# A fused attention, mixture and convolution kernel on one core: taps of the convolution by DMA, half banks for the first scores, no unread products, other numbers in the planner

## The chip, the cores and the metric

The kernel runs on one core of one Trainium2 chip. The metric is the device time of one execution in microseconds (us), lower is better. Three executions of the kernel before took 445.81, 446.19 and 446.75 us (median 446.19). The execution that the profiler recorded took 444.8 us, of which its trace spans 443.0 us.

A core has a matrix engine (PE; its weight loads are listed as PEld), a vector engine (DVE), a scalar engine (ACT), a general engine (POOL) and a queue engine (SP) that issues most DMAs. Each engine runs its own instructions in order and waits on semaphores for the others. PE's results land in PSUM, a memory of 8 banks; everything else lies in SBUF.

## The reference

Everything is float32: batch B = 4, H = 8 heads of 64, S = 576 tokens, 512 channels.

```python
def reference(**kw):
    x = attention(q, k, v)          # (4, 8, 576, 64), window of 64 keys
    x = x.transpose(0, 2, 1, 3).reshape(4, 576, 512)
    x = channel_mix(x); return gated_conv(x)

def attention(q, k, v):
    s = (q @ k.T) / 8               # masked: 0 <= query - key < 64, else -1e9
    s = s - s.max(-1); e = exp(s)
    return (e / (e.sum(-1) + 1e-9)) @ v

def channel_mix(x):
    xp = x shifted by one token (zero at the start of each batch)
    xk = mu_k * x + (1 - mu_k) * xp
    xr = mu_r * x + (1 - mu_r) * xp
    h = relu(xk @ w_k)              # 512 -> 1024
    return sigmoid(xr @ w_r) * ((h * h) @ w_v)

def gated_conv(x):
    gate = sigmoid(sum over k = 0..4 of conv_w[k] * x shifted by 4 - k tokens)
    return (gate * (x @ w_val)) @ w_out
```

## The kernel before, in words

**First stage.** The 2304 tokens are cut into five blocks t = 0..4 of 256, 512, 512, 512 and 512 tokens, and each block into four pairs of heads: 20 units, numbered u = 4t + pair. A unit goes through these steps: scores on PE (`qk`, L289), scaling and window mask on DVE (`mask`, L301), a fix for batch starts on POOL (L311), the row maximum on DVE (`top`, L319), the exponentials with their sums on ACT (`exp`, L325), reciprocal and scaling on DVE (L332, L334), transposes on PE (`tp`, L342), their copies to SBUF on ACT or DVE (`pt`, L348 and L349), the product with v on PE (`pv`, L355), and a copy of its result to the block's transposed x (L361, L362).

From x a block mixes four operands: for each half g of the channels and each of r and k, x is scaled (L393 on ACT, L398 on DVE), the shifted x is added (`xm`, L409 on DVE), and for the blocks after the first the sum is split into a rounded high part (L423 on ACT, L424 on DVE) and the rest as low part (L426 on DVE). Then come the products r (4 tiles), h (8 tiles) and v (4 tiles). In block 0 they are plain float32 products with 256 columns (L457); in blocks 1 to 4 each is three passes (high by high, high by low, low by high) of 512 columns (L439). The split operands of block 1 lie where block 0's weights lay (`wide_x`), so they can be written only when block 0's products are done. In block 0 the weights themselves are made ready on ACT and DVE (`words`, `weight`: L210 to L239).

**Second stage.** Batch by batch (b = 0..3): x is read back (`load`, L569), split into the operands of a seven-product scheme (`prep`, L594 to L604), multiplied by w_val (L672), the products are combined and multiplied by the gate (L684 to L718), the result is split into high and low parts (g0h, g0l, g1h, g1l: L423, L424, L426) and multiplied by w_out (L439, names `out`), and stored (L746, L747). The gate of a batch has for each half p of the channels: tap 0 on ACT (L624), the other taps on DVE (L626), and the sigmoid on ACT (L653). For the taps in `BY_DMA`, in batches 1 to 3, ACT scales the shifted x into a buffer `tt` instead (L632; two such buffers exist), and POOL issues a DMA that adds the buffer to the gate (L643); the taps on DVE come behind that addition.

**What sets the order.** All operations are registered with the class `Plan`, each with an engine (or a choice of two), an assumed duration, a rank and its dependencies. `run` simulates the engines with these durations and emits the operation that can start first, among near ties the one of lowest rank. The tables `RANK` and `ADJ` give the ranks. The engines then run their instructions in the emitted order. PSUM rings limit what may be in flight: one buffer of two banks for scores (`pq`), two banks for transposes and `pv` (`pa`), four for r, h and v (`pg`). Where the simulation finds PE without work for over 700 ns before the first r product, `fill` (L882 to L888) emits products of the identity with itself whose result nothing reads.

## Time and profile before

| what | value |
|---|---|
| three executions | 445.81, 446.19, 446.75 us |
| profiled execution | 444.8 us, span 443.0 us |
| PE | 424.6 us busy (96%), 3172 records |
| DVE | 326.6 us busy (74%), 474 records |
| ACT | 266.2 us busy (60%), 584 records |
| POOL | 22.4 us busy (5%) |
| chain that ended last | PE 71%, DVE 20%, issue 3%, DMA 3%, ACT 2% |
| granted TensorE clock | mean 1.0 of full speed |

The busy time of an engine is the union of its records. The chain is followed back from the last instruction, at each step to what released it. Records of one engine overlap a little, so that the distance from one start to the next is a few hundredths of a microsecond less than a duration.

### The profile page before, as it was taken

To read this page: it belongs to the slowest core of one execution; us is meant where nothing else is said; L and a number is where in the kernel's file an instruction comes from. 1 tells how busy PE (TensorE), PEld (TensorE's weight loads), DVE (VectorE), ACT (ScalarE), POOL (GpSimd) and SP (SyncE) were. 2 spreads that over 40 slices of the span, in tenths; PEclk is the share of its full clock that TensorE was granted. 3 is DMA by queue.
4 is the path that set the end of the run, shared out by engine and by line. 5 is a ranking of instruction groups with operands and counts; after the bars stand their busy time and mean duration, and the time that the engine had idled before them with its cause. 6 is when DMAs were issued, how large, how long until landed. Compare 5 with 4: busy or idle time off the path is not lost.

```text
span 443.0 us, 7915 instructions
## 1 busy us (share of the span) xinstructions
PE 424.6 (96%) x3172; PEld 362.1 (82%) x3172; DVE 326.6 (74%) x474; ACT 266.2 (60%) x584; POOL 22.4 (5%) x69
## 2 busy tenths in 40 slices
PE   6879999899999999999999999999999799999996
PEld 4668788778878888888888878888889799899996
DVE  3999999998496149588147277765992899999950
ACT  4799987777546257896138553366430877685321
POOL 2001010011010001000000000000000001010000
PEclk9999999999999999999999999999999999999999
DMA  8998551602230143210121007300426426552022
GB/s 302 415 371 300 211 176 58 209 8 65 70 106 24 55 167 106 83 57 25 48 73 48 0 1 255 124 14 0 139 99 208 108 56 134 187 120 95 28 108 80
DMA packets 16692, 52.44 MB, mean 118 GB/s; under 512 B 1936, under 2 KB 2704, under 8 KB 15120
## 3 DMA queue, kind: packets, MB, share of 16 engines
q1 hardware_dynamic: 14928, 42.10, 27.5%
q0 software_dynamic: 864, 3.54, 4.0%
q10 hardware_dynamic: 864, 6.29, 3.8%
q8 instruction: 25, 0.41, 0.4%
q14 instruction: 11, 0.09, 0.1%
HBM read 38.95 MB, written 9.44 MB: 109 GB/s over the span
## 4 chain that ended last, share of the span: by engine, by line
PE 71%; DVE 20%; issue 3%; DMA 3%; ACT 2%; POOL 1%; ACTq 0%; POOLq 0%
PE h L439 20%; PE v L439 20%; PE r L439 9%; PE out L439 8%; PE qk L289 3%; PE at L355 3%; DMA xb<-x2d 3%; PE at L342 3%; PE val3m L672 3%; DVE x L604 2%; DVE m L319 2%; DVE words L215 2%; DVE s L301 2%; DVE s L334 1%; DVE xt L594 1%
## 5 line engine op out<-in xcount | busy, mean ns | idle before, releaser
L439 PE MATMUL h<-x,wk 128*128 128x512 f32 x384 | 91.3, 393 | 0.0
L439 PEld LDWEIGHTS h<-x,wk 128*128 128x128 f32 x384 | 71.0, 188 | 14.6
L439 PE MATMUL v<-sh,wv 128*128 128x512 f32 x256 | 80.5, 391 | 0.0
L325 ACT ACTIVATE s<-s,m 128x128 f32<-128x128 f32 x144 | 55.8, 388 | 12.4 <-DVE m L319 12.2
L439 PEld LDWEIGHTS v<-sh,wv 128*128 128x128 f32 x256 | 48.1, 188 | 10.3 <-issue 0.3
L439 PE MATMUL v<-sl,wv 128*128 128x512 f32 x128 | 49.9, 390 | 0.0
L439 PE MATMUL r<-x,wr 128*128 128x512 f32 x192 | 47.2, 397 | 0.7 <-DVE x L426 0.7
L439 PEld LDWEIGHTS r<-x,wr 128*128 128x128 f32 x192 | 35.1, 188 | 8.8 <-DVE x L426 1.1
L626 DVE SCALAR_TENSOR_TENSOR gate<-xb,wc,gate 128x576 f32<-128x576 f32 x52 | 39.5, 810 | 0.0
L516 DVE TENSOR_TENSOR sl<-rk,sh 128x1024 fp32r<-128x1024 f32 x16 | 19.5, 1222 | 21.7 <-ACT rk L514 21.7
L485 ACT ACTIVATE rk<-h 128x512 f32<-128x512 f32 (+1 forms) x35 | 19.3, 560 | 26.4 <-PE h L439 25.7
L301 DVE SCALAR_TENSOR_TENSOR s<-qk,cap 128x1024 f32<-128x1024 f32 (+1 forms) x24 | 22.5, 953 | 14.9 <-PE qk L289 8.7
L539 DVE TENSOR_TENSOR sgs<-v,sgs 128x512 f32<-128x512 f32 (+1 forms) x20 | 12.7, 635 | 25.7 <-PE v L439 25.7
L439 PEld LDWEIGHTS v<-sl,wv 128*128 128x128 f32 x128 | 24.0, 188 | 4.8
L439 PE MATMUL out<-g0h,wr 128*128 128x288 f32 x128 | 27.4, 295 | 0.0
L439 PE MATMUL out<-g1h,wr 128*128 128x288 f32 x128 | 27.2, 295 | 0.0
L355 PEld LDWEIGHTS at<-pt,vt 128*64 128x64 f32 x576 | 19.9, 137 | 8.6 <-issue 3.8
L325 ACT ACTIVATION_READ_ACCUMULATOR s<-s,m 128x1 f32 x144 | 26.9, 187 | 0.0
L355 PE MATMUL at<-pt,vt 128*64 128x64 f32 x576 | 23.6, 226 | 2.3 <-ACT pt L348 1.9
L409 DVE SCALAR_TENSOR_TENSOR xm<-xT,omu,xm 128x320 f32<-128x320 f32 (+6 forms) x56 | 25.4, 516 | 0.0
L342 PE MATMUL at<-ident,s 128*128 128x128 f32 x144 | 22.6, 278 | 2.1 <-DVE s L334 0.8
L319 DVE TENSOR_REDUCE m<-s 128x8 f32<-128x1024 f32 (+1 forms) x20 | 22.1, 1106 | 2.0 <-POOL s L311 1.9
(125 smaller groups left out, 762.9 us busy)
## 6 DMA issues: line engine op xcount, KB each, us to landing
qk<-qk SPq DMA_DIRECT2D x16, 544.0 KB, 4.9
vt<-vh SPq DMA_DIRECT2D x16, 512.0 KB, 4.0
xb<-x2d SPq DMA_DIRECT2D x4, 1152.0 KB, 6.5
out_t<-st SPq DMA_DIRECT2D x15, 288.0 KB, 2.1
x2d<-sgs SPq DMA_DIRECT2D x16, 256.0 KB, 2.0
gate<-tt POOLq DMA_DIRECT2D x6, 576.0 KB, 4.8
words<-w_r SPq DMA_DIRECT2D x2, 1024.0 KB, 8.6
words<-w_k ACTq DMA_DIRECT2D x2, 1024.0 KB, 7.6
```

What stands on the lines that cost most here:

```text
L289: PE.matmul(a["ps"][heads[c % 2], h, c // 2 * P:c // 2 * P + P], lhsT=a["q"][heads[h], c * W:(c + 1) * W], rhs=a["k"][heads[h], c * W:c * ...
L301: V.scalar_tensor_tensor(out=o, in0=ps[:, i:i + j], scalar=D ** -0.5, in1=cap[:, None, :].to_broadcast([P, j, P]), op0=ALU.mult, op1=ALU.min)
L319: V.tensor_reduce(out=l(0), in_=a["s"], axis=AX.X, op=ALU.max, negate=True)
L325: ACT.activation(out=s, in_=s, func=AF.Exp, bias=l(0)[:, c:c + 1], accum_out=l(1)[:, c:c + 1])
L342: PE.transpose(a["tp", h][:, c * P:(c + 1) * P], a["s"][:, h * n2 + c, :], ident)
L355: PE.matmul(a["o"][heads[h], c * W:(c + 1) * W], lhsT=a["v"][:, c, heads[h]], rhs=a["pt"][:, h, c * W:(c + 1) * W], start=True, stop=True)
L409: V.scalar_tensor_tensor(out=m, in0=xT[:, f, lo:hi], scalar=omu[:, c:c + 1], in1=m, op0=ALU.mult, op1=ALU.add)
L439: PE.matmul(ps, lhsT=a, rhs=b[:, kt, :], start=(kt == 0 and i == 0), stop=(kt == nk - 1 and i == 2))
L485: ACT.activation(out=o, in_=ps, func=AF.Relu)
L516: lambda E: E.tensor_tensor(out=Ss[t][1][:, f, :n], in0=rk(), in1=f32(Ss[t][0][:, f, :n]), op=ALU.subtract))
L626: V.scalar_tensor_tensor(out=g, in0=src, scalar=c, in1=g, op0=ALU.mult, op1=ALU.add)
L672: PE.matmul(z[bank][:, j, :HS], lhsT=lhs, rhs=rhs, start=new and kt == 0 and e == 0, stop=kt == 1 and e == 2, skip_group_check=not new)
```

## The change

- `BY_DMA` is `(3, 4)` instead of `(4,)`: in batches 1 to 3 two taps are scaled by ACT and added by DMA, and the taps 1 and 2 stay on DVE. The two additions to one half of a gate are made one after the other.
- The scores of the first block no longer use the `pq` buffer. Two pools of one bank each, `q00` and `q01`, hold one head's scores of two units side by side: unit `hp` uses columns 256 * (hp % 2) and following of both. Two units are in flight (`pq0=2`). The pools are closed, and `pq` is opened, where unit 4 starts; that unit waits for the masks of units 2 and 3. The mask of a first-block unit is two instructions as before.
- `fill`, its call and its products are gone.
- The planner's assumed durations are changed (`mm_ns`, `words`, `qk`, `pv`, `xm`, `mask`), it now stretches a PE operation by `COLD` where PE was busy for under half of the `SPAN` ns before, and `RANK` and `ADJ` hold other numbers. The order on every engine changes.

```diff
-BY_DMA = (4,)
+BY_DMA = (3, 4)
...
-RANK = {'first': -699, 'unit': 87, 'mix': -174, 'w_r': -349, 'w_k': -177, 'w_v': 83, 'halves': 554, 'next': -181,
+RANK = {'first': -656, 'unit': 1, 'mix': -1509, 'w_r': -700, 'w_k': -340, 'w_v': 192, 'halves': 692, 'next': -234,
...
-    WAIT, PASS = 700, 480
     TABLE = 1280
+    SPAN, COLD = 4000, 1.75
...
-            if w[0] == "pe" and self.fill and t - free.get("pe", 0) > self.WAIT:
-                self.fill(t, int((t - max(free.get("pe", 0), 1500) - 250) // self.PASS))
-            free[w[0]] = t + w[1]
-            end[key] = t + w[1]
+            ns = w[1]
+            if w[0] == "pe":
+                work = [(a, b) for a, b in work if b > t - self.SPAN]
+                ns *= self.COLD if sum(b - max(a, t - self.SPAN) for a, b in work) < self.SPAN / 2 else 1
+                work.append((t, t + ns))
+            free[w[0]] = t + ns
+            end[key] = t + ns
...
-    mm_ns = lambda n: n / 2.4 + (12 if n > HS else 13)
+    mm_ns = lambda n: n / 2.4 + (18 if n > HS else 13)
...
-    pq = pas.enter_context(tc.tile_pool(name="pq", bufs=1, space=PSUM, side="right"))
     pa = pas.enter_context(tc.tile_pool(name="pa", bufs=2, space=PSUM, side="right"))
-
-    plan = Plan(pg=4, pq=1, pa=2, valu=1, valv=1, pc=2)
+    p0s = ExitStack()
+    qk0 = [p0s.enter_context(tc.tile_pool(name=f"q0{h}", bufs=1, space=PSUM, side="right")) for h in range(2)]
+
+    plan = Plan(pg=4, pq=1, pq0=2, pa=2, valu=1, valv=1, pc=2)
...
-            a["ps"] = pq.tile([P, 2, TB], F32, tag="qk", name=f"qk{u}")
+            if t:
+                if "pq" not in Q:
+                    p0s.close()
+                    Q["pq"] = pas.enter_context(tc.tile_pool(name="pq", bufs=1, space=PSUM, side="right"))
+                a["ps"] = Q["pq"].tile([P, 2, TB], F32, tag="qk", name=f"qk{u}")
+                ps = [a["ps"][:, h] for h in range(2)]
+            else:
+                if "qk0" not in Q:
+                    Q["qk0"] = [q.tile([P, TB], F32, tag="qk", name=f"qk{u}{h}") for h, q in enumerate(qk0)]
+                ps = a["ps"] = [q[:, hp % 2 * TA:][:, :TA] for q in Q["qk0"]]
...
-        op(("qk", u), "pe", 115 * nc_ + 200, r[0], [("ldqk", u)], qk, ring=("pq", ("mask", u)))
+        op(("qk", u), "pe", 104 * nc_ + 200, r[0],
+           [("ldqk", u), *([("mask", 2), ("mask", 3)] if u == HP else [])], qk, ring=("pq" if t else "pq0", ("mask", u)))
...
-    idle = {}
-
-    def fill(t, n):
...
-        for _ in range(n):
-            PE.matmul(idle["ps"][:, :P], lhsT=ident, rhs=ident, start=True, stop=True)
-    plan.fill = fill
```

What this moves, at three places. Line numbers of the new kernel differ: its scores are L302 (before L289), masks L315 (L301), maxima L333 (L319), scalings L348 (L334), `xm` L423 (L409), splits L438 and L440 (L424, L426), taps on DVE L640 (L626).

The first is the start of DVE. In the names, `qk0` to `qk3` of before are the score buffers of units 0 to 3, `qk00` and `qk01` of the new kernel its two banks; `s0`, `m0` belong to units 0 and 1, `s2`, `m2` to units 2 and 3. Before:

```order
L301 SCALAR_TENSOR_TENSOR s0_156<-qk0_146,cap_94 128x256 x2
L319 TENSOR_REDUCE m0_174<-s0_156 128x4
L301 SCALAR_TENSOR_TENSOR s0_156<-qk1_164,cap_94 128x256 x2
L319 TENSOR_REDUCE m0_174<-s0_156 128x4
L301 SCALAR_TENSOR_TENSOR s2_199<-qk2_184,cap_94 128x256 x2
L319 TENSOR_REDUCE m2_214<-s2_199 128x4
L301 SCALAR_TENSOR_TENSOR s2_199<-qk3_205,cap_94 128x256 x2
L332 RECIPROCAL m0_174<-m0_174 128x4
```

And in the new kernel:

```order
L315 SCALAR_TENSOR_TENSOR s0_166<-qk00_146,cap_94 128x256
L315 SCALAR_TENSOR_TENSOR s0_166<-qk01_147,cap_94 128x256
L315 SCALAR_TENSOR_TENSOR s0_166<-qk00_146,cap_94 128x256
L315 SCALAR_TENSOR_TENSOR s0_166<-qk01_147,cap_94 128x256
L333 TENSOR_REDUCE m0_186<-s0_166 128x4 x2
L315 SCALAR_TENSOR_TENSOR s2_201<-qk00_146,cap_94 128x256
...
L333 TENSOR_REDUCE m2_213<-s2_201 128x4 x2
L346 RECIPROCAL m0_186<-m0_186 128x4
```

Masks and maxima alternated unit by unit; now two units are masked, then their two maxima follow, and so on for the other two (the lines left out are masks of the same kind).

The second is DVE where block 1's operands are made (`x_881` before, `x_978` now; `xm` is the mixed block, `s8` to `s11` are scores of units 8 to 11). Before:

```order
L301 SCALAR_TENSOR_TENSOR s9_859<-qk9_731,cap_94 128x1024
L334 TENSOR_TENSOR s8_720<-s8_720,m8_799 128x1024
L424 CAST x_881<-xm_70 128x1024
L426 TENSOR_TENSOR x_881<-xm_70,x_881 128x1024
L539 TENSOR_TENSOR sgs_72<-v_0_0_715,sgs_72 128x256
L398 TENSOR_SCALAR xm_70<-xT_95,sm_59 128x512 x2
L301 SCALAR_TENSOR_TENSOR s10_924<-qk10_884,cap_94 128x1024
...
L319 TENSOR_REDUCE m9_969<-s9_859 128x8
L426 TENSOR_TENSOR x_881<-xm_70,x_881 128x1024 x2
```

And in the new kernel:

```order
L348 TENSOR_TENSOR s9_784<-s9_784,m9_841 128x1024
L315 SCALAR_TENSOR_TENSOR s10_897<-qk10_812,cap_94 128x1024
...
L333 TENSOR_REDUCE m10_941<-s10_897 128x8
...
L348 TENSOR_TENSOR s10_897<-s10_897,m10_941 128x1024
L438 CAST x_978<-xm_70 128x1024
L440 TENSOR_TENSOR x_978<-xm_70,x_978 128x1024 x2
L315 SCALAR_TENSOR_TENSOR s11_1017<-qk11_921,cap_94 128x1024
...
L440 TENSOR_TENSOR x_978<-xm_70,x_978 128x1024 x2
```

Units 9 and 10 are finished, and unit 11 is masked, before the last two low parts; in the old order units 9 and 10 stood behind them with their scalings, and unit 11 with its mask.

The third is DVE in the second stage, at the taps of batch 2 (`gate2`) beside the input of batch 3 (`xb3`). Before:

```order
L626 SCALAR_TENSOR_TENSOR gate2_3276<-xb2_2977,wc_61,gate2_3276 128x576
L715 TENSOR_TENSOR gate1_3097<-sgs_72,gate1_3097 128x2x288 x2
L426 TENSOR_TENSOR g1l_3030<-gate1_3097,g1h_3029 128x576 x2
L426 TENSOR_TENSOR g0l_3028<-gate1_3097,g0h_3027 128x576
L626 SCALAR_TENSOR_TENSOR gate2_3276<-xb2_2977,wc_61,gate2_3276 128x576
L594 TENSOR_TENSOR xt_2544<-xb3_3433 128x576
```

And in the new kernel:

```order
L440 TENSOR_TENSOR g1l_3017<-gate1_3085,g1h_3016 128x576
L640 SCALAR_TENSOR_TENSOR gate2_3269<-xb2_2964,wc_61,gate2_3269 128x576 x4
L729 TENSOR_TENSOR gate2_3269<-sgs_72,gate2_3269 128x2x288
L608 TENSOR_TENSOR xt_2545<-xb3_3415 128x576
L608 TENSOR_TENSOR xt_2545<-xt_2545,xb3_3415 128x576
```

The taps of one half of a gate now stand as one run of four (two channel tiles by two taps) behind both additions of that half.

## Rows read from the trace of the kernel before

**Rows 1.** The page's part 1: busy time, share of the span, instructions.

```profile
PE 424.6 (96%) x3172; PEld 362.1 (82%) x3172; DVE 326.6 (74%) x474; ACT 266.2 (60%) x584; POOL 22.4 (5%) x69
```

**Rows 2.** The chain that ended last: start us, length us, what.

```profile
89.09 1.24 DVE s L334
...
316.91 21.76 PE v L439 x96
...
378.83 7.00 DMA xb<-x2d
```

**Rows 3.** Timeline of PE at the start: start, length, instructions, idle time before.

```profile
4.25 1.13 PE L289 MATMUL qk<-qk 64*64 64x128 f32 x16
...
23.89 1.10 PE L289 MATMUL qk<-qk 64*64 64x128 f32 x32
24.92 0.71 PE L888 MATMUL idle<-ident 128*128 128x128 f32 x4
27.30 1.13 PE L457 MATMUL r<-x,words 128*128 128x256 f32 x4 [1.67 <-DVE x L409]
```

**Rows 4.** Timeline of DVE at the start, same columns.

```profile
5.52 0.76 DVE L301 SCALAR_TENSOR_TENSOR s<-qk,cap 128x256 f32<-128x256 f32 x2 [4.52 <-PE qk L289]
...
11.66 0.76 DVE L301 SCALAR_TENSOR_TENSOR s<-qk,cap 128x256 f32<-128x256 f32 x2 [0.37 <-PE qk L289]
...
26.77 0.87 DVE L409 SCALAR_TENSOR_TENSOR x<-xT,omu,x 128x256 f32<-128x256 f32 x2
27.56 1.22 DVE L301 SCALAR_TENSOR_TENSOR s<-qk,cap 128x1024 f32<-128x1024 f32 x1
```

**Rows 5.** Timeline of DVE where the second block's input is split.

```profile
77.88 0.69 DVE L424 CAST x<-xm 128x1024 fp32r<-128x1024 f32 x1
...
81.88 1.66 DVE L409 SCALAR_TENSOR_TENSOR xm<-xT,omu,xm 128x320 f32<-128x320 f32 x4
...
84.66 2.36 DVE L426 TENSOR_TENSOR x<-xm,x 128x1024 fp32r<-128x1024 f32 x2
```

**Rows 6.** Timeline of PE over the same stretch, up to the second block's h.

```profile
85.94 4.15 PE L439 MATMUL r<-x,wr 128*128 128x512 f32 x17 [0.72 <-DVE x L426]
90.46 0.63 PE L342 MATMUL at<-ident,s 128*128 128x128 f32 x4 [0.37 <-DVE s L334]
90.84 3.00 PE L439 MATMUL r<-x,wr 128*128 128x512 f32 x12
...
96.95 1.15 PE L355 MATMUL at<-pt,vt 128*64 128x64 f32 x32
98.03 1.19 PE L439 MATMUL h<-x,wk 128*128 128x512 f32 x4
```

**Rows 7.** Groups of instructions by line: busy us, mean ns, idle before.

```profile
L626 DVE SCALAR_TENSOR_TENSOR gate<-xb,wc,gate 128x576 f32<-128x576 f32 x52 | 39.5, 810 | 0.0
...
L632 ACT ACTIVATE tt<-xb,wc 128x576 f32<-128x576 f32 x12 | 8.6, 764 | 0.0
```

**Rows 8.** Timeline of PE around 260 us.

```profile
257.92 1.15 PE L355 MATMUL at<-pt,vt 128*64 128x64 f32 x30 [0.48 <-ACT pt L348]
...
261.15 1.15 PE L355 MATMUL at<-pt,vt 128*64 128x64 f32 x30 [0.43 <-ACT pt L348]
```

**Rows 9.** Timeline of PE in the last stage.

```profile
348.67 3.46 PE L672 MATMUL val0m<-x,wk 128*128 128x288 f32 x24 [2.00 <-ACT sgs L684]
...
354.10 6.79 PE L672 MATMUL val1m<-x,wk 128*128 128x288 f32 x48 [0.38 <-DVE sgs L713]
...
387.60 1.87 PE L672 MATMUL val2m<-x,wk 128*128 128x288 f32 x12 [1.06 <-ACT sgs L684]
```

**Rows 10.** Timeline of ACT in the last stage.

```profile
347.98 0.63 ACT L684 ACTIVATE sgs<-val0m 128x576 f32<-128x576 f32 x1
...
386.92 0.63 ACT L684 ACTIVATE sgs<-val2m 128x576 f32<-128x576 f32 x1
```

**Rows 11.** DMA issues: transfers, KB each, median us from issue to landing.

```profile
gate<-tt POOLq DMA_DIRECT2D x6, 576.0 KB, 4.8
```

More of the change, by code (lines that the diff above doesn't have):

```diff
@@ new lines @@
+RANK = {'first': -656, 'unit': 1, 'mix': -1509, 'w_r': -700, 'w_k': -340, 'w_v': 192, 'halves': 692, 'next': -234,
+        'nextstep': 10, 'att': -55, 'step': 1, 'inner': 11, 'ahead': 1346, 'mixes': -631, 'mixstep': 84, 'prep': -273,
+        'gate': 2097, 'ldx': 1343, 'w2': -1020, 'out': 69, 'gated': 1250, 'early': 151, 'late': 683}
+ADJ = {('h', 0, 4, 0): 15, (('w_v', 2), 'hi'): -215, ('mask', 1): -445, ('pv', 18): 150,
+       (('w_k', 2), 'lo'): -80, ('h', 0, 3, 0): 270, ('r', 3, 3): 330, (('w_v', 0), 'g'): 565,
+       ('valc', 0, 1, 0): -245, ('out', 0, 1, 0, 0): -150, ('norm', 3): -90, ('out', 0, 1, 1, 0): 250,
+       ('slo', 0, 3): -10, ('top', 6): 140, ('r', 0, 3, 0): -115, ('exp', 2): -260, ('r', 0, 1): 70,
+       ('out', 3, 1, 1, 0): -15, ('exp', 7): -15, (('w_k', 3), 't'): 100, ('wc0', 't'): -185,
+       ('out', 2, 1, 1, 0): -280, ('xsum', 1, 6): -250, ('xhi_', 1, 3): -55, ('val', 3, 'm1'): -250,
+       ('part', 1, 0, 3): -105, ('val', 2, 'm1'): 250, ('rec', 4): 10, ('tp0', 9): 95,
+       (('w_r', 0), 'ld'): 345, ('r', 0, 0, 0): -100, ('out', 3, 0, 1, 0): -100, ('v', 0, 0): 100,
+       ('xsum', 1, 5): -30, ('exp', 3): -20}
@@ L62 @@
     RAMP, SLOW = 7500, 1.6
-    WAIT, PASS = 700, 480
     TABLE = 1280
+    SPAN, COLD = 4000, 1.75
     def __init__(self, **rings):
-        self.ops, self.rings, self.fill = [], rings, None
+        self.ops, self.rings = [], rings
     def op(self, key, eng, ns, rank, deps, fn, ring=None, table=None, moves=0):
@@ L88, in run @@
         used = {r: [] for r in self.rings}
+        work = []
         table = None
-        link = 0
+        link = 700
         while ready:
@@ L297, in mask @@
             s = a["s"] = half("s", [P, 2 * TB // P, P])[:, :2 * n2, :]
-            ps = a["ps"].rearrange("p h (c j) -> p (h c) j", j=P)
-            for i, j in [(0, 2 * n2)] if n == TB else [(0, n2), (TB // P, n2)]:
-                o = s[:, i and n2:][:, :j]
-                V.scalar_tensor_tensor(out=o, in0=ps[:, i:i + j], scalar=D ** -0.5,
-                                       in1=cap[:, None, :].to_broadcast([P, j, P]), op0=ALU.mult, op1=ALU.min)
-        op(("mask", u), "dve", v_ns(n * 2), r[1], [("qk", u), "cap", *back("mask", 1), *back2("tp")], mask)
+            full = a["ps"].rearrange("p h (c j) -> p (h c) j", j=P) if t else None
+            for i in range(1 if t else 2):
+                o, x = (s, full) if t else (s[:, i * n2:(i + 1) * n2], a["ps"][i].rearrange("p (c j) -> p c j", j=P))
+                V.scalar_tensor_tensor(out=o, in0=x, scalar=D ** -0.5,
+                                       in1=cap[:, None, :].to_broadcast([P, 2 * n2 if t else n2, P]), op0=ALU.mult, op1=ALU.min)
+        op(("mask", u), "dve", v_ns(n * 2) + (0 if t else 160), r[1], [("qk", u), "cap", *back("mask", 1), *back2("tp")], mask)
         firsts = [c for c in range(nc_) if (t0 // W + c) % (S // W) == 0]
@@ L876, in tile_kernel @@
                 out_pair(b, h, p, s + RANK["out"] + 10 * (2 * h + p))
-    idle = {}
-    def fill(t, n):
-        if any(k in Ps for k in [("r", 0, m) for m in range(NF)]) or n <= 0 or "stop" in idle:
-            return
-        if "ps" not in idle:
-            idle["ps"] = pg.tile([P, TB], F32, tag="g", name="idle")
-        for _ in range(n):
-            PE.matmul(idle["ps"][:, :P], lhsT=ident, rhs=ident, start=True, stop=True)
-    plan.fill = fill
     with tc.manual_schedule():
```

20 lines of the change are left out of this document (4 added, 16 removed).

## The prediction

> **What bounds the kernel now.** I read the busy times first: PE is busy 96% of the span, DVE 74%, ACT 60% [rows 1]. So a saving counts only where PE stands idle or where something holds PE up. The chain of waits says where that is: up to about 90 us it runs through DVE (its last DVE link is a scaling of scores at 89.09), then through PE almost without a break to 338, where only the last stage has links of a DMA, DVE and ACT again, the last of them the load of x for the last batch at 378.83 [rows 2]. I then looked for PE's idle time in its timelines. At the start PE is underfed: its first 16 score products take 1.13 us at 4.25, while 32 of them take 1.10 us at 23.89, so the array ran at half rate at first, and its first r product starts at 27.30 [rows 3]. Later the idle pieces are few: 0.72 us behind a split at 85.94 and 0.37 behind a scaling at 90.46 [rows 6], 0.48 and 0.43 near 260 [rows 8], and 2.00, 0.38 and 1.06 in the last stage [rows 9]. Outside these, PE's work is not changed by the edit: r, h, v, val and out have the same products, at 21.76/96 = 0.227 us each for the 512-wide ones [rows 2].
>
> **The start: half banks.** Before, DVE does its four mask rounds at a step of (11.66 - 5.52)/3 = 2.05 us [rows 4]; a round has a mask of 0.76 and a maximum of about as much, so some 0.6 us a round, 2 us in all, are spent waiting for PE. The change puts two units in flight, which could take that out. But a unit's scores fill half of each of two banks, and the other half belongs to the next unit, and the masks in the built program wait for both. Worked through: unit 0's scores from 3.85 (0.4 before their 4.25, since no unread products stand ahead), unit 1's behind them to 5.8 (1.13 us a unit at half rate, less what overlaps, [rows 3]), first mask 5.85 against 5.52; units 2 and 3 are scored only after the masks have read the banks, to 7.8 and 9.9; their masks end near 11.3, their maxima 12.5. The first reciprocal then stands near 12.5; before, it followed the fourth mask, at 11.66 + 0.76 = 12.4 [rows 4]. The exponentials come later, the last unit's by some 2 us, which DVE covers with weight conversions. I take the first mix at 27.3 against 26.77 [rows 4], and the first r product at 28.2 against 27.30 [rows 3]. Bounds: DVE could be 2.2 us earlier if nothing waited, or 2 us later if the last exponentials hold up the transposes.
>
> What the row shows is that the mask waits for PE's scores: idle 4.52 us, ended by them [rows 4]. The Trainium skill, "PSUM — Partial Sum Buffer", section "PSUM bank collisions raise a hardware error", says that two engines must not be in one bank and quadrant at the same time, even at different addresses, and that guards go by bank. By that rule the half bank gives the first mask no earlier start than the end of unit 1's scores; without it the gain would be the 2.2 us of the rival below. No run here shows a collision, and the sum stands on the waits alone.
>
> **The start: other order.** What ends last before 90 us is the low part of block 1's r operand: PE waits for it at 85.94, the end of DVE's split begun at 84.66 [rows 5, 6]. Counting DVE's instructions ahead of that split in both orders, the new one has one more 1024-wide mask, one more maximum, two more scalings and one more low part: 5 x 1.14 = 5.7 us (1.22 less the overlap of 0.08 by which the next record starts early, [rows 4]); and one more set of four `xm`, 1.58 us [rows 5]. Two more 512-wide copies against one 512-wide square and one weight cast less I take as cancelling. So 7.3 us more DVE work come first, and the split ends at 85.8 + 7.3 = 93.1, or 92.4 if the 0.7 us that DVE waits in short pieces between 27 and 86 go too. Behind it PE has 42 of the 48 r products (six need only the first half's operand) and two sets of four transposes before the first h of block 1: 42 x 0.227 + 2 x 0.38 [rows 6] = 10.3 us, so h starts at 102.7 to 103.4, against 98.03 [rows 6].
>
> That is not all loss, since PE meanwhile does attention that came later before: two more units transposed (four sets of 0.38 to 0.49, together 1.5 to 1.9), one more `pv` (98.03 - 96.95 = 1.08) and one more set of scores (24.92 - 23.89 = 1.03) [rows 3, 6]: 3.6 to 4.0. Net: 102.7 - 98.03 - 4.0 = +0.7 to 103.4 - 98.03 - 3.6 = +1.8. PE itself would be ready: from its first r product at 28.2 its own work to that point is 68 us with the same steps, so with 3 us of idle time h could start at 99.
>
> **The removed products.** 36 records of the unread kind go, at 24.92 four of them in 0.71 us [rows 3]. PE is not the limit there, so by themselves they give nothing back. Without them the array may be at half rate until r runs. Price from rows: the attention of units 1 to 3 at the start and the first r products (8 x 0.22 us at full rate) doubled is 1 to 4 us of PE time, of which DVE's work hides most. I take +0.7, from 0 to +3. Start in all: 1.2 + 0.7 = +1.9 (from -2.2 to +5).
>
> **The middle.** Around 260 PE waits twice for a copy on ACT, 0.48 and 0.43 us, with about as much in shorter pieces between [rows 8]. In the new order the last units' transposes and `pv` stand between h and v products, so there is other work for PE: I take -0.9, from -1.6 to +1 (a new gap elsewhere).
>
> **The last stage.** Twelve DVE taps of 0.81 go (9.7 us by duration, [rows 7]); ACT gets twelve more scalings of 0.76 = 9.2 us [rows 7], POOL six more adding DMAs at 4.8 us to landing [rows 11]. But the DVE time is worth only what PE loses to DVE there: 0.38 [rows 9]. The 2.00 us at 348.67 is ACT's copy at 347.98, queued behind x for another batch [rows 9, 10]; the new order has a wider conversion and two scalings ahead of a copy in that place, so I take +0.2. The 1.06 at 387.60 is ACT's copy at 386.92 behind the conversion that waits for the last x, issued 378.83 after the taps of the batch before last were done [rows 2, 9, 10]. With fewer taps on DVE that DMA can go some 4 us earlier, its 7.00 us then end by 382, and the gap goes: -1.1. What is late next is the gate: each half needs ACT's scalings, two DMAs in series, (4.8 + 0.9) x 2 = 11.4 us [rows 11], with 0.9 for the issue, and the taps behind them in DVE's queue, with the low parts that PE waits for queued behind those taps. For the last batch that puts the second half's operand near 423, two us before PE wants it; if DMAs that overlap take half as long again, 2 x 2.4 us, the slack is gone and 2 to 3 us are lost. I take +1.0 for it and 0 for the 0.38: last stage 0.2 - 1.1 + 1.0 = +0.1, from -2 to +3.
>
> **Sum.** +1.9 - 0.9 + 0.1 = +1.1 on the profiled execution's 444.8, 445.9. The median of the runs shown, 446.19, is 1.4 above that execution, so the forecast as a median is 447.3. About 0.2% (0.9 us) is what a measurement of this kernel can tell from no change.
>
> **Rivals.**
> (a) Faster, by the masks: the guards let unit 1's scores be written while unit 0 is masked, and DVE loses nothing in the four rounds. Place: DVE before 13 us. Price: 2.2 us off everything up to 93, since that stretch is DVE's [rows 2]. For it: the step of 2.05 us is longer than DVE's work in it [rows 4]; against it: both units share the banks. It decides if the first mix starts before 26 us. Then the start is 1.9 - 2.2 = -0.3, and the time 446.2 - 0.3 - 0.9 + 0.1 = 445.1; with a last stage of -1.1 (no late gates) 443.9, which I take.
> (b) No difference: the change does not do what it says; the half banks and taps only shift waits, and start +1, middle -0.9 and last stage 0 cancel: 446.2.
> (c) Clearly slower, by the array's rate: the unread products kept it at full rate from about 13 us, and without them it stays at half rate until r has run for a while. For it: half rate at 4.25 [rows 3]; against it: DVE bounds that stretch. Price +3 in place of my 0.7: 447.3 + 2.3 = 449.6. The Trainium skill, "TensorE: Matmul & The Clock Gate", section "Part 1: The HAM clock gate", says the throttled state is the default and sustained activity releases it; the rows at 4.25 and 23.89 agree, and by the rule this rival holds.
> (d) Clearly slower, by the gates: the two DMAs in series make the last batches' gates late, 2 to 3 us in place of my 1.0: 449.
>
> **Chances.** Forecast (446.0 to 448.6) 0.41; (a) 0.28; (b) 0.12; (c) 0.11; (d) 0.08. Of the forecast's own range some 40% lies within 0.2%, 0.16; with (b) that is 0.28. Faster is (a), 0.28; slower is the rest, 0.25 + 0.11 + 0.08 = 0.44. The range takes (a) down to 443.3 and (c) and (d) up to 450.4.
>
> **What would show it.** Right: first mask at 5.8 or later and four masks before 11.5; the first mix near 27.3; PE's h of block 1 at 102 to 104; no wait of PE on ACT's copies near 260; the last x issued near 375 and no gap before the third val product set; PE waiting for a g operand near 425 by at most 1 us. Wrong: first mix before 26 (a), granted clock low past 28 us with r products at twice 0.22 (c), PE waits of 2 us and more on g operands (d), or h of block 1 by 100, which would mean that DVE's added 7.3 us were not on the path.

## The result

| | kernel before | changed kernel |
|---|---|---|
| median of 4 executions each, one chip | 446.00 us | 451.79 us (450.25 to 452.4) |
| ratio | | 1.0123 [1.0107, 1.0139] |
| profiled execution | 444.8 us, span 443.0 | 451.51 us, span 449.4 |

The changed kernel is slower by 5.8 us by the medians, and by 5.5 us, 1.2%, by the ratio. The sign was forecast; the size was not: 451.79 lies above the 447.3 and above the end of the range, 450.4. One execution of the runs below, 455.85 us of s14_exps_tail, counts as a slow one and is left out of its numbers.

The changed kernel's busy times, first part of its page (busy us, share of the span, records):

```profile
PE 421.1 (94%) x3136; PEld 360.2 (80%) x3136; DVE 308.9 (69%) x444; ACT 287.8 (64%) x612; POOL 25.8 (6%) x79
```

Beside [rows 1], PE and DVE are busy for less time and ACT for 21.6 us more: the span grew by waits. I place them by three rows of PE's timeline in the changed kernel: the first h of block 1, the end of the first stage (from the chain that ended last), and the first product of the last stage.

```profile
97.76 8.44 PE L453 MATMUL r<-x,wr 128*128 128x512 f32 x36
107.70 0.63 PE L356 MATMUL at<-ident,s 128*128 128x128 f32 x4 [1.50 <-DVE s L348]
...
111.30 1.87 PE L453 MATMUL h<-x,wk 128*128 128x512 f32 x7
```

```profile
324.34 21.76 PE v L453 x96
```

```profile
356.06 3.46 PE L686 MATMUL val0m<-x,wk 128*128 128x288 f32 x24 [1.96 <-ACT sgs L698]
359.35 1.76 PE L686 MATMUL val1m<-x,wk 128*128 128x288 f32 x12
361.75 6.83 PE L686 MATMUL val1m<-x,wk 128*128 128x288 f32 x48 [0.64 <-DVE sgs L727]
```

Block 1's h starts at 111.30 against 98.03 [rows 6], 13.3 us later. PE has by then done 3.6 to 4.0 us of attention that came later before (the prediction's count), so the first part costs **+9.3 to +9.7** here. The last v ends at 346.1 against 338.67 [rows 2]: +7.4, so the middle gave back some 2.1. The span ends +6.4, so the last stage gave back 1.0. These are differences of two single executions; what such a difference is worth, the experiments show. In the last stage PE still waits 1.96 and 0.64 (2.00 and 0.38 in [rows 9]); the third wait of [rows 9], 1.06, is gone.

What the 9.5 us are made of shows in the busy time of DVE up to the end of the split that block 1's r needs (before, r waited for it). Kernel before, then changed kernel (stretch, its length, DVE's busy time and records, granted clock of PE, DMA share, GB/s):

```profile
0.00:12.40 12.40, 5.23 (x13) 1.00 0.86 317
12.40:36.00 23.60, 23.33 (x45) 1.00 1.00 393
36.00:59.60 23.60, 23.42 (x31) 1.00 0.60 199
59.60:77.20 17.60, 17.53 (x28) 1.00 0.40 137
77.20:85.80 8.60, 8.60 (x13) 1.00 0.69 216
sum 85.80, DVE 78.11; mean DVE 15.62
```

```profile
0.00:12.30 12.30, 5.47 (x14) 1.00 0.86 306
12.30:41.80 29.50, 28.15 (x52) 1.00 0.93 365
41.80:73.00 31.20, 28.31 (x38) 0.95 0.52 173
73.00:90.10 17.10, 15.00 (x21) 1.00 0.46 148
90.10:99.20 9.10, 8.90 (x14) 1.00 0.41 123
sum 99.20, DVE 85.83; mean DVE 17.17
```

The cuts are the same events in both: the first reciprocal, the end of block 0's r, the first v product, the last v product. The split ends 13.4 us later. Of that, 85.83 - 78.11 = 7.7 us is more work, and (99.20 - 85.83) - (85.80 - 78.11) = 5.7 us is more waiting. Before, DVE waited for almost nothing behind its first reciprocal (0.27 + 0.18 + 0.07); now 1.35, 2.89 and 2.10.

The changed kernel's r does not wait for this split: PE comes to r only at 97.76, and the split ends, at 99.2, about when the six r products end that do not need it. What holds PE up ahead of h is another scaling, in the chain that ended last:

```profile
106.33 1.24 DVE s L348
107.70 0.63 PE at L356 x4
```

Three of DVE's waits before the split, in the changed kernel's timeline of DVE:

```profile
55.55 0.70 DVE L217 TENSOR_SCALAR words<-words 128x1024 int32<-128x1024 int32 x1 [1.42 <-DMA words<-w_v]
...
70.05 0.69 DVE L363 COPY pt<-at 128x512 f32<-128x512 f32 x1 [1.44 <-PE at L356]
...
88.54 0.42 DVE L553 TENSOR_TENSOR sgs<-v,sgs 128x256 f32<-128x256 f32 x1 [1.78 <-PE v L471]
```

It waits for PE, and PE waits for it. PE's timeline over the middle of that stretch:

```profile
60.10 1.99 PE L471 MATMUL h<-x,words 128*128 128x256 f32 x8 [1.50 <-DVE rk L501]
63.62 1.06 PE L356 MATMUL at<-ident,s 128*128 128x128 f32 x8 [1.53 <-ACT words L214]
65.27 2.07 PE L369 MATMUL at<-pt,vt 128*64 128x64 f32 x32 [0.58 <-DVE pt L363]
67.27 1.64 PE L302 MATMUL qk<-qk 64*64 64x128 f32 x32
```

and the waits of PE over the whole of the changed kernel, by what was waited for (total us, times, longest):

```profile
PE at L356 <- DVE s L348: 8.8, 3, 3.7
PE qk L302 <- DMA qk<-qk: 4.5, 2, 3.6
PE at L369 <- DVE pt L363: 2.1, 4, 0.7
PE val0m L686 <- ACT sgs L698: 2.0, 1, 2.0
```

The three waits for scalings are in the first part: 3.60 at 13.25, 3.71 at 20.92 and 1.50 at 107.70. The first is no loss: before, the same transposes start at 13.37, and the time ahead of them goes to unread products.

### The profile page after: what moved, and what is told of

Same layout as the page of the kernel before. It is cut to its first block, busy times and chain, and to the rows that moved or that the text cites. A ratio compares the mean times of both kernels' runs of the same rounds, so it can differ in the third digit from the quotient of the medians.

```text
span 449.4 us, 7859 instructions
## 1 busy us (share of the span) xinstructions
PE 421.1 (94%) x3136; PEld 360.2 (80%) x3136; DVE 308.9 (69%) x444; ACT 287.8 (64%) x612; POOL 25.8 (6%) x79
## 4 chain that ended last, share of the span: by engine, by line
PE 82%; DVE 9%; DMA 4%; ACT 2%; issue 1%; SPq 0%; POOL 0%; ACTq 0%; DVEq 0%
PE v L453 20%; PE h L453 20%; PE out L453 11%; PE r L453 8%; PE qk L302 4%; PE at L369 4%; PE at L356 3%; PE v L471 3%; PE val3m L686 3%; PE val2m L686 2%; PE val1m L686 2%; DMA words<-w_v 2%; DVE xm L423 1%; DMA xb<-x2d 1%; DVE s L315 1%
## 5 line engine op out<-in xcount | busy, mean ns | idle before, releaser
L453 PE MATMUL v<-sh,wv 128*128 128x512 f32 x256 | 81.9, 393 | 0.0
L369 PEld LDWEIGHTS at<-pt,vt 128*64 128x64 f32 x576 | 21.7, 149 | 11.2 <-ACT pt L362 3.9
L315 DVE SCALAR_TENSOR_TENSOR s<-qk,cap 128x1024 f32<-128x1024 f32 (+1 forms) x24 | 22.4, 952 | 11.8 <-PE qk L302 7.0
L356 PEld LDWEIGHTS at<-ident,s 128*128 128x128 f32 x144 | 17.3, 146 | 16.3 <-issue 9.4
L640 DVE SCALAR_TENSOR_TENSOR gate<-xb,wc,gate 128x576 f32<-128x576 f32 x40 | 30.3, 812 | 0.0
L369 PE MATMUL at<-pt,vt 128*64 128x64 f32 x576 | 25.4, 238 | 4.0 <-DVE pt L363 2.1
L362 ACT ACTIVATE pt<-at 128x512 f32<-128x512 f32 (+1 forms) x30 | 16.5, 560 | 18.9 <-PE at L356 18.4
L302 PE MATMUL qk<-qk 64*64 64x128 f32 x576 | 23.7, 306 | 5.0 <-DMA qk<-qk 4.5
```

The lines of the kernel that those rows point to most:

```text
L302: PE.matmul(ps[h][heads[c % 2], c // 2 * P:c // 2 * P + P], lhsT=a["q"][heads[h], c * W:(c + 1) * W], rhs=a["k"][heads[h], c * W:c * W + P ...
L315: V.scalar_tensor_tensor(out=o, in0=x, scalar=D ** -0.5, in1=cap[:, None, :].to_broadcast([P, 2 * n2 if t else n2, P]), op0=ALU.mult, op1= ...
L356: PE.transpose(a["tp", h][:, c * P:(c + 1) * P], a["s"][:, h * n2 + c, :], ident)
L362: ("act", a_ns(n), lambda h=h: ACT.activation(out=a["pt"][:, h, :n], in_=a["tp", h][:, :n], func=AF.Copy)),
L369: PE.matmul(a["o"][heads[h], c * W:(c + 1) * W], lhsT=a["v"][:, c, heads[h]], rhs=a["pt"][:, h, c * W:(c + 1) * W], start=True, stop=True)
L453: PE.matmul(ps, lhsT=a, rhs=b[:, kt, :], start=(kt == 0 and i == 0), stop=(kt == nk - 1 and i == 2))
```

## The experiments

In the replays the planner's choice is taken out and a written list of the operations, each with its engine, is emitted instead; each starts from the list that the planner made for one of the two kernels:

```diff
-        while ready:
-            ...
+        for key, eng in ORDER:
+            ...
+            next(w for w in ops[repr(key)][3] if w[0] == eng)[2]()
```

Times are medians. Ratios are to the kernel before, run beside each on the same chip, with 95% intervals; its medians there were 445.6 to 446.2.

**Parts of the change, one at a time.** *No unread products*, in the kernel before:

```diff
-    plan.fill = fill
```

> The kernel before without its unread products, order unchanged. My theory after the result: the loss comes from the planned order of the first block's work on ACT and DVE, so this changes little: 445.3 to 447.3 us. Rival (c), the array's clock: without the products PE stays at half rate until r runs, and this alone costs most of the loss: 449 us or more.

Measured 446.10, 1.0011 [0.9997, 1.0026]. The array does run slow without them, as its timeline of PE shows, where 32 scores take 1.99 (1.10 in [rows 3]) and the first four r products 2.07 (1.13):

```profile
24.76 1.99 PE L289 MATMUL qk<-qk 64*64 64x128 f32 x32
28.21 2.07 PE L457 MATMUL r<-x,words 128*128 128x256 f32 x4 [1.46 <-DVE x L409]
```

The first r starts 0.9 us later, and the end moves by no more than the interval allows, -0.1 to +1.2 us. Rival (c), priced at +3, falls.

*Half banks*, in the kernel before, with the new order of the first scores, masks and maxima only:

```diff
+    qk0 = [p0s.enter_context(tc.tile_pool(name=f"q0{h}", bufs=1, ...)) for h in range(2)]
```

> The kernel before with the first block's scores in half banks and the changed kernel's order of the four scores, masks and maxima; unread products kept, every later instruction in the order of before. Theory (planned order): 445.5 to 447.3 us, the first mix within 0.6 us of 26.8. Rival (a), half banks save the waits of the mask rounds: 444 us. Rival, half banks cost: 448 or more.

Measured 445.58, 1.0002 [0.9988, 1.0016]. Its first reciprocal stands at 12.23, its first mask at 6.35 and its first mix at 27.52 (26.77 in [rows 4], expected within 0.6 of 26.8); in the time nothing is gained and nothing lost. Rival (a) falls.

*Two taps by DMA*, the kernel before, its planner and its tables:

```diff
-BY_DMA = (4,)
+BY_DMA = (3, 4)
```

> The kernel before with two taps by DMA and nothing else, so that only the last stage is planned anew. Theory (planned order of the first block): 444.8 to 447.2 us. Rival (d), the DMAs in series make the gates late: 448 us or more, with PE waiting for a low part of g near 425.

Measured 447.68, 1.0046 [1.0030, 1.0062]: 2 us slower, between the two expectations. Its waits of PE have one that the kernel before does not have, at 429.98, for a low part of the gated values:

```profile
PE out L439 <- DVE g0l L426: 0.9, 1, 0.9
```

So a late gate as in rival (d) exists where the tables were not made for two taps, worth 0.9 us in this execution. Of the 3.1 us by which the profiled span is longer (446.1 against 443.0), 2.0 stand already at block 1's h (100.05 against 98.03), where the instructions on every engine are those of the kernel before; the last stage adds 1.1. The difference in the first part goes with PE's granted clock, which in the kernel before is 1.00 from 28 to 36 us. Here (stretch, length, PE's busy time and records, granted clock, DMA share, GB/s):

```profile
28.00:32.00 4.00, 3.56 (x38) 0.72 1.01 415
32.00:36.00 4.00, 4.00 (x17) 0.86 1.01 415
```

So one execution of an order can differ from another by 2 us at that h, and how much of the measured 2 us the taps cost stays open.

*The same with the new kernel's order of the last stage*, the old order up to it:

```diff
-ORDER = before
+ORDER = before[:turn_s] + rest of the new order      # two taps
```

> The kernel before in its own order until all of v is done, then the last stage of the changed kernel, with two taps by DMA in its order. By the PE idle of the two profiles in that stage (4.7 us before, 3.5 after) 444.5 to 445.5 us; if two taps by DMA cost by themselves, as in the run with the taps alone, 447 to 448 us.

Measured 446.03, 0.9988 [0.9967, 1.0010], between the two expectations. In the new order the taps cost nothing, and gain nothing that shows. None of the kernels run is faster than the kernel before; this one equals it.

**Where in the program: new order first, old order behind.** The new kernel's list up to one operation, then the rest as in the kernel before, with one tap by DMA:

```diff
+ORDER = new[:r(0,0)] + rest of old     # s16_start
+ORDER = new[:h(0,1)] + rest of old     # s17_h
+ORDER = new[:v(0,1)] + rest of old     # s18_v
+ORDER = new[:h(1,0)] + rest of old     # s8_reverse
```

> The changed kernel (half banks, no unread products) in its own order up to the first r product of block 0, from there the order of before with one tap by DMA. By PE's idle time in the two profiles the first 28 us cost 1.5 us: 447 to 448.5 us. If the order of the first four units is the cause (exponentials in the order 0, 2, 3, 1) with all that follows from it: 450.5 us or more.

> The same with the seam at the first product of h tile 1 of block 0 (near 48 us in the changed kernel). By the idle time to there +3 us: 448 to 450 us. If the stretch from r to h is the cause (mixes of block 0 late, w_r's buffers released late, w_v's loads late): 451 us or more while the seam at r gives 448 or less.

> The same with the seam at block 0's first v product (near 73 us). By the idle time to there +6 to +7.5 us: 451.5 to 454 us, most of the 8 of the seam at block 1's h. If the stretch between v and block 1 makes the loss: 449 us or less.

> The reverse: the changed kernel (half banks, no unread products) in its own order up to the first h product of block 1, and from there what is left in the order of before, with one tap by DMA. Theory: 451.5 to 455 us, the whole loss and none of the later regain. Rival, the loss comes from the later parts: 446 to 448.5 us.

| new order up to | time | ratio | first product of the last stage, profiled execution |
|---|---|---|---|
| nothing (kernel before) | 446.00 | 1 | 338.51 |
| block 0's r (s16_start) | 447.76 | 1.0039 [1.0027, 1.0050] | 340.98 |
| block 0's second h (s17_h) | 451.14 | 1.0106 [1.0075, 1.0136] | 343.26 |
| block 0's v (s18_v) | 458.80 | 1.0293 [1.0262, 1.0324] | |
| block 1's h (s8_reverse) | 453.91 | 1.0173 [1.0142, 1.0205] | 347.88 |
| all (the changed kernel) | 451.79 | 1.0123 [1.0107, 1.0139] | 345.94 |

By the ratios the start to the first r costs 1.7 us (1.2 to 2.2), up to block 0's second h it is 4.7 (3.3 to 6.1), up to block 1's h 7.7 (6.3 to 9.1), and the rest of the new order gives some 2 us back. s16_start and s8_reverse came as expected; s17_h came out by its second alternative, a loss between r and h. The loss is in the first part, as in the ledger read from the trace, but 7.7 and not 9.5 us: the last column, like the ledger, is from single executions, that of s17_h being the fastest of its four (448.44, the others 451.11 to 451.63) and that of s8_reverse the slowest. How the steps divide is no better known than the intervals say, and s16_start has small waits of its own behind its seam (0.54 at 38.34 and 0.34 at 40.68, both for ACT), so that even the 1.7 is not the start's alone. s18_v, a miss, stands out of the row. In it PE waits 3.01 us for DVE's `words` ahead of v, a wait that neither order has, so a cut there measures the seam.

**Old order first, new order behind**, two taps:

```diff
+ORDER = old[:r(0,0)] + rest of new     # s15_start
+ORDER = old[:r(1,0)] + rest of new     # s1_splice
+ORDER = old[:h(1,0)] + rest of new     # s7_splice
```

> The opposite at the first seam: the kernel before (its score buffers, its unread products) in its own order up to the first r product of block 0, then what is left in the changed kernel's order, two taps by DMA. If the loss is made behind the start, as the idle time says: 449 to 451.5 us. If the start is the cause: 446 us or less.

> The kernel before (its score buffers, its unread products) in its own order up to the first r product of block 1, and from there everything left in the order of the changed kernel, with two taps by DMA. Theory: the changed kernel is about 9 us late by block 1's h and regains about 3 later, so this is faster than both: 442.5 to 444.5 us. If the loss lay behind the first block, 448 us or more; if the regain is only slack that a late start leaves behind, 445.5 to 446.5.

> The kernel before in its own order up to the first h product of block 1 (unlike the splice before, with block 1's r products inside that part), and from there what is left in the changed kernel's order, with two taps by DMA. Theory: 443.5 to 446 us, since the lateness is all in the part that is replaced. Rival, taps and later order cost too (the taps alone cost 0.5% in the order of before): 447 to 449 us.

Measured 453.64, 1.0171 [1.0150, 1.0192]; 454.01, 1.0199 [1.0180, 1.0219]; 456.20, 1.0225 [1.0207, 1.0244]. All three are slower than their theories said, and the timelines of PE of the last two say why: one wait each at the seam. First s1_splice, then s7_splice:

```profile
90.57 1.94 PE L512 MATMUL at<-ident,s 128*128 128x128 f32 x8 [6.40 <-DVE s L504]
```

```profile
113.13 1.94 PE L512 MATMUL at<-ident,s 128*128 128x128 f32 x8 [9.57 <-DVE s L504]
```

The new order counts on units whose scalings the old order does later. 6.40 and 9.57 us are made by the splice and are no part of the change, so neither run says what a good first part is worth. s15_start has a wait of 3.21 us for a mask at 29.59 (0.40 in the kernel before); its loss is the seam's and that of the part behind it together.

**One suspect of the first part at a time**, in the changed kernel.

*Unit 10's attention behind block 1's splits* (the work that the prediction had put on the path), moved back:

```diff
-(('top', 10), 'dve') ... (('norm', 10), 'dve')      # ahead of the splits
+(('top', 10), 'dve') ... (('norm', 10), 'dve')      # behind (('xlo', 1, 1, 'k'), 'dve')
```

> The changed kernel in its own order, but unit 10's maximum, exponentials, scaling, transposes and product with v stand behind the last split of block 1's operands instead of ahead of block 1's first r product. Theory now: the new order pulls attention forward to places where ACT and DVE cannot deliver it and PE waits; this gives back 1.5 to 3 us of the changed kernel's 451.8: 448.8 to 450.3 us, with PE's first h of block 1 before 109.5. Rival, the loss is not in this order but in the two taps: unchanged, 451 to 452.5 us.

Measured 459.28, 1.0303 [1.0280, 1.0327], a miss: PE now waits 5.46 us for that unit's scaling at 108.02. The new wait is longer than what the move could have saved, so the run does not price the old place.

*w_v's conversions and the squares ahead of the exponentials of unit 7*:

```diff
-(('exp', 7), 'act')      # behind h of block 0
+(('exp', 7), 'act')      # behind (('top', 8), 'dve')
```

> The changed kernel in its own order, except between the end of block 0's h products and its first v products: the conversions of w_v and the squares of relu stand ahead of the exponentials of unit 7 on ACT, the relus ahead of two low parts on DVE, and PE runs the first v product before unit 7's transposes. Theory (ACT delivers the inputs of v too late, PE idles and its clock falls): v starts near 65 us instead of 73.0, the time is 446.5 to 449.5 us. Rival, that stretch is set by the late loads of w_v (landed at 55.5) or by DVE's work alone: v starts after 70, 450.5 us or more.

Measured 458.41, 1.0278 [1.0261, 1.0295], a miss. v starts at 68.55 as wanted (72.95 in the changed kernel), and then PE waits 3.24 us at 81.42 for a scaling, a wait that the move made.

*Block 1's first mixes later*:

```diff
-(('xm', 1, 0, 'r'), 'dve')      # ahead of h(0,1)
+(('xm', 1, 0, 'r'), 'dve')      # behind (('pt', 7, 1), 'dve')
```

> The changed kernel in its own order, but the first two mixes of block 1 stand behind the maxima and scalings of units 8 and 9 (the scaled half on DVE instead of ACT), so that the exponentials of units 6 and 7 can start some 3 us earlier. Theory of the units' order: the loss is older than this place, so little comes back: 450 to 453 us. Rival, the early mixes are what holds PE up between 58 and 66 us: 447 to 449.5 us.

Measured 455.97, 1.0217 [1.0192, 1.0242]: worse, a miss. The waits near 60 and 64 (1.50, 1.54 and 0.58) stay, so the early mixes do not make them; new are 1.57 for a mask at 74.12 and 1.79 for `words` at 82.83.

*Exponentials of the first units in the order 0, 1, 2, 3* (the new kernel has 0, 2, 3, 1), and the same with the old last stage and one tap:

```diff
-(('exp', 2), 'act') ... (('exp', 3), 'act') ... (('exp', 1), 'act')
+(('exp', 1), 'act') ... (('exp', 2), 'act') ... (('exp', 3), 'act')
```

> The changed kernel in its own order, but the exponentials, sums, reciprocals and scalings of units 1, 2 and 3 change places, so that they come in the order 0, 1, 2, 3 in which PE transposes the units; the changed kernel has 0, 2, 3, 1. Theory now: with 0, 2, 3, 1 unit 1's scaling comes last (20.1 us), its transposes wait 3.7 us and units 2 and 3 queue behind it on PE, x of unit 3 is ready at 31.4 instead of near 23, block 0's mixes end 5 us later, and everything that waits for block 0's r products (the buffers of w_r, the conversions of w_k, the loads of w_v) follows. So this gives back 3 to 6 us: 446 to 449 us, no wait of PE over 2 us near 21. Rival, the start is covered by weight conversions as I predicted, and the loss is made between 40 and 75 us by itself: 450.5 us or more.

> As the kernel with the units in order 0, 1, 2, 3, but the last stage from the second buffers on is that of before: its order, with one tap by DMA. If two taps by DMA cost as they did alone (0.46%, 2 us), this is 1 to 2.5 us faster than the kernel with the units in order; if the changed kernel's last stage is the better one (its PE idle there sums to about 1 us less), it is 0.5 to 1.5 us slower.

Measured 452.93 (449.95 to 455.14), 1.0138 [1.0099, 1.0178], and 450.89 (449.08 to 453.89), 1.0105 [1.0069, 1.0141]: the rival's time for the first. The wait of 3.71 at 20.92 is gone, and two others stand in s12_exps' timeline of PE:

```profile
21.30 1.12 PE L534 MATMUL at<-pt,vt 128*64 128x64 f32 x16 [2.67 <-DVE pt L528]
...
28.58 1.98 PE L467 MATMUL qk<-qk 64*64 64x128 f32 x32 [2.43 <-DVE s L480]
```

The two runs against each other are inconclusive, their intervals overlap. But their instructions are the same on every engine up to the last stage, and yet block 1's h starts at 115.02 in the profiled execution of s12_exps, the slowest of its six (455.14), and at 109.62 in that of s14_exps_tail. In the latter the second wait is 0.78:

```profile
27.59 1.10 PE L467 MATMUL qk<-qk 64*64 64x128 f32 x32 [0.78 <-DVE s L480]
```

With the longer wait PE's granted clock was 0.80 in 25 to 30 us and 0.52 in 30 to 35; with the shorter one it was 1.00 in both. So a wait read from one execution of this order need not be in the next, and 109.62 against the changed kernel's 111.30 does not show that the move gains.

*The granted clock kept up*, by unread products in PE's idle time at 58 to 64 us:

```diff
+('FILL', 6),      # ahead of h(0,3)
+('FILL', 7),      # behind it
```

> The changed kernel in its own order, with 13 unread identity products added: 6 ahead of the relu products h of block 0's last two units and 7 behind them, where PE idles between 58 and 64 us. They change nothing that is kept. Theory 1, the fall of the granted clock to 0.66 at 65 to 70 us belongs to the loss: in that stretch 32 products of 1.64 us for a slab go at half rate, so with the clock kept 1 to 1.8 us come back, about 450.2 us. Rival: the wait behind (PE waits for the norms and the values anyway, v starts at about 73 us whatever the scores cost) swallows it: 451.5 to 452.3 us, with the granted clock near 1.0 in 60 to 75 us and the idle time before v longer. Second rival: the products push the scores back without keeping the clock, 452.5 us or more.

Measured 452.44 (451.05 to 452.92), 1.0142 [1.0114, 1.0169]. Its time lies between those of its two rivals (452.3 and 452.5). In the profiled execution the clock did as wanted. Changed kernel, then this one (stretch, length, PE's busy time and records, granted clock, DMA share, GB/s):

```profile
60.00:65.00 5.00, 3.06 (x16) 1.00 0.00 0
65.00:70.00 5.00, 4.67 (x72) 0.66 0.33 87
```

```profile
60.00:65.00 5.00, 4.46 (x30) 1.00 0.00 0
65.00:70.00 5.00, 3.90 (x80) 1.00 0.38 93
```

Block 1's h starts at 110.39, 0.9 earlier, and val0m at 345.03, 0.9 earlier, but the span ends at 449.3 against 449.4: the last stage waits in other places (0.43 at 413.06 is one). That execution is the fastest of its six. By the mean granted clock of each execution, the two at 1.00 took 451.05 and 451.24 us and the four at 0.996 took 452.43 to 452.92; of the changed kernel, the one at 1.00 took 450.25 and the three at 0.994 took 451.51 to 452.40. So a fall of the clock goes with 1 to 2 us, and the added products did not keep the clock up in most executions. It is not the main loss: the kernel before at 1.00, 22 executions beside the runs here, took 444.21 to 445.79, so that some 5 us remain with the clock up. Which comes first, PE's idle time or the fall, these runs do not separate.

*The chain from block 0's last r product to the loads of w_v made shorter*:

```diff
+(('r', 0, 1), 'pe')            # behind (('r', 0, 3), 'pe'), not behind h(0,0)
+((('w_r', 1), 'lo'), 'dve')    # ahead of (('norm', 4), 'dve')
+((('w_v', 2), 'ld'), 'act')    # behind (('pt', 4, 1), 'act')
```

> The changed kernel in its own order but for the chain from block 0's r products to the loads of w_v: the last r tile follows the other three at once, w_r's last low part comes ahead of the scalings of units 4 and 5, and the conversions of the last two pieces of w_k and the loads of w_v behind them come as early as that allows. Theory 1, this chain is what makes the first part late: r done near 39.5 us (41.8 in the changed kernel), the first of the two loads issued near 43.5 (47.1), the 1.42 us that DVE waits for w_v near 55 gone, first v product at 70 to 71.5 us (72.95), block 1's split 1 to 2.5 us earlier, and 449.3 to 450.8 us. Rival, the order on the in-order engines takes it back: PE or ACT waits for the scalings of units 4 and 5, which come 1.2 us later, the first v product stays at 72.5 to 74 us, and the time is 451.3 to 453.5.

Measured 452.55 (450.73 to 453.45), 1.0133 [1.0096, 1.0171]: the rival's time. The chain did get shorter: r done at 39.3 (41.8), the first load issued at 42.81 (47.11), no wait of DVE for w_v any more, the first v at 72.25 (72.95). In its place PE waits 1.00 at 43.60 for ACT and 1.53 at 64.27 for a scaling, and DVE waits 1.20 at 46.84 for a transpose.

## Why the prediction was wrong

**The step that failed** is the start's other order, where the prediction says "the split ends at 85.8 + 7.3 = 93.1, or 92.4 if the 0.7 us that DVE waits in short pieces between 27 and 86 go too". The count of work was right, 7.3 against the 7.7 measured. The step carried the old order's waits over into the new one: I let DVE's idle time stay at what it was or fall. It rose by 5.7 us, and the split ended at 99.2. In a stretch where DVE is busy for 49.55 of 49.8 us before, this cannot be seen in the trace of before: it is idle time that the new order makes. The prediction counted instructions of the new order on DVE alone. From 99.2 its own 10.3 us would still have given h at 109.5; h came at 111.30, and the wait of 1.50 at 107.70 is most of the rest.

**"PE itself would be ready ... with 3 us of idle time h could start at 99"** failed with it. The 68 us are PE's busy time in the kernel before between the same two points, without the 3.6 to 4.0 us of attention that the prediction itself adds there; with them its own sum gives 103. Measured, changed kernel and then kernel before (stretch, length, PE's busy time and records, granted clock, DMA share, GB/s):

```profile
28.20:111.30 83.10, 75.11 (x771) 0.98 0.50 169
```

```profile
27.30:98.03 70.73, 68.17 (x672) 1.00 0.52 184
```

PE had 75.1 us of work and was idle for 8.0, not 3. Ahead of that stretch it waited 3.71 us at 20.92, where unit 1's transposes stand behind a scaling that starts at 20.09, and in it 1.50, 1.53 and 0.58 between 58 and 66. The first mix came at 27.94 (forecast 27.3) and the first r product at 29.39 (28.2). "The exponentials come later ... which DVE covers with weight conversions" is the same error: DVE was covered, PE was not.

**What is behind the extra waits.** They lie in a loop of in-order queues: DVE waits for PE's transposes and v products, PE for DVE's scalings and ACT's copies, ACT for both. That the loop makes the loss is read from the traces, not shown by a run. Six moves each took a wait, or some work, from its place (unit 10, v's start, the mixes, the exponentials, the clock, the loads of w_v), and none gave back time that can be told from the spread: four kernels came at 452 to 456 (450.89 for the exponentials with the old last stage), two at 458 and 459. In executions with a mean granted clock of 0.999 or more the changed kernel took 450.25 (one execution) and the moves 449.08 to 455.82; the two fastest, 449.08 and 449.95, have the exponentials in order, too few to tell a gain of 1 us. Where a move made a wait of its own (3 us and more for unit 10 and for v's start) it says nothing on the old place. ACT is a rival that no run separates: it had 76.8 us of work up to the split, 67.0 before, and the prediction has no term for that. Which instruction, if any, starts the loss stays open. Shown is that the new order of the first part, with what comes with it there, carries the loss: 7.7 us (6.3 to 9.1) up to block 1's h, some 1.7 of them with the cut at the first r.

**Half banks**, taken as no gain: right, by the time (1.0002) and by the mechanism. The first mask starts at 5.74 (forecast 5.85), and the first reciprocal at 12.21 (12.5). PE's first scores of both units end at 5.62, and the first mask follows them:

```profile
5.74 0.76 DVE L315 SCALAR_TENSOR_TENSOR s<-qk,cap 128x256 f32<-128x256 f32 x2 [4.74 <-PE qk L302]
```

The Trainium skill ("PSUM — Partial Sum Buffer", section "PSUM bank collisions raise a hardware error") has the guards go by bank and not by address; this start, behind both units' scores, agrees, and no run here shows a collision.

**Removed products**, +0.7 from 0 to +3: measured +0.5 us [-0.1, +1.2] alone. Slow scores and r products, as the row of 2.07 shows, cost no more than that in the kernel before, where the chain that ended last still has a link of DVE at 89.09 [rows 2]. The Trainium skill ("TensorE: Matmul & The Clock Gate", section "Part 1: The HAM clock gate") says that the throttled state is the default; the 1.99 and 2.07 without the products agree.

**The middle**, -0.9: about -2.1 between the two profiled executions, right in sign and larger than the end of its range, -1.6. The waits of [rows 8] are gone; where they stood, one `pv` runs without a wait:

```profile
263.62 1.15 PE L369 MATMUL at<-pt,vt 128*64 128x64 f32 x32
264.70 3.02 PE L453 MATMUL r<-x,wr 128*128 128x512 f32 x12
```

**The last stage**, +0.1: -1.0 between the two profiled executions, inside its range; by the times of s2_tail, which has this stage alone, -1.5 to +0.4. The +1.0 for late gates did not come: there is no such wait in the changed kernel, though an adding DMA takes 5.7 us (4.8 in [rows 11]). The -1.1 came, but not by the way that I gave. The last x is issued at 384.82 (forecast 375; before 378.83), 1.4 us earlier if one takes off the 7.4 by which this kernel runs behind, not 4. ACT's copy of val2m no longer stands behind a conversion that waits for x, as in [rows 10]; it waits for the product itself:

```profile
386.23 0.65 ACT L698 ACTIVATE sgs<-val2m 128x576 f32<-128x576 f32 x1 [0.26 <-PE val2m L686]
```

**The sum.** +1.9 - 0.9 + 0.1 was forecast; +9.5 - 2.1 - 1.0 = +6.4 of span was measured between the profiled executions. The first term is the one that puts the time outside the range, and its bound is wrong too: "from -2.2 to +5" had no place for waits that a new order makes.

## What to carry to other kernels

When a change emits a new order on engines that feed each other, the work added ahead of the critical instruction need not be all of its delay (here 7.7 of 13.4 us); each queue has to be walked with its waits, since idle time of the new order is in no trace of the old one. How much to allow for that is not shown here; what is shown is that a stretch where DVE was busy for 49.55 of 49.8 us can gain some 4.9 us of waits (2.89 + 2.10 + 0.20, less 0.18 + 0.07). Replaying one order up to a cut and the other behind it finds the stretch that loses, if the seam is looked at first: a wait that neither order has makes the time worthless. And a place read from one execution of each kernel wants a second one: here the same instructions reached block 1's h 2.0 and 5.4 us apart.

## What the runs showed beyond that

In the changed kernel the granted clock of PE was 0.66 in 65 to 70 us, that is, at its lower level (1.2 of 2.4 GHz) for part of them, after a stretch of 5 us in which PE was busy for 3.06; 32 scores then took 1.64 us instead of 1.10. In s14_exps_tail's profiled execution PE was busy for 2.88 us of the same stretch and the clock stayed at 1.00. Filling the idle time kept it at 1.00 in the profiled execution, and the median was no lower (452.44 against 451.79).

Two units' scores in the two halves of a bank, with masks that wait for both, cost nothing against the kernel before's one buffer of two banks (445.58 against 445.86).

With twelve adding DMAs in place of six their median time to landing was 5.7 us in the changed kernel, 5.3 in s2_tail, where the time did not change, and 4.8 in e1_taps, as before: their number alone does not set it.
